# Moving the small steps of a softmax from ACT and GpSimd to VectorE, from the fourth block on

## The chip, the cores and the metric

The kernel runs on one core of a Trainium2 chip. The core has five engines, each with its own queue of instructions that it works off strictly in order: TensorE (PE in the profile; its weight loads are PEld) multiplies matrices and writes into PSUM, VectorE (DVE) and ScalarE (ACT) read and write SBUF and PSUM, GpSimd (POOL) works on SBUF, and SyncE (SP) issues the transfers (DMA). An instruction that needs another engine's result waits on a semaphore at the head of its queue, and everything behind it in that queue waits too. The metric is the time of one execution on the device in microseconds, lower is better.

## The reference, cut to what matters

```python
def sm(a, b):                                   # scale = 1/sqrt(128)
    s = scale * (a @ b.transpose(0, 2, 1))
    s = s - s.max(-1, keepdims=True)
    e = np.exp(s)
    return e / (e.sum(-1, keepdims=True) + 1e-09)
agent_v = sm(agents, k) @ v                     # 49 agents, 12480 tokens, width 128
x = sm(q, agents) @ agent_v                     # per token: a softmax over 49 scores
h = x @ w_in                                    # 128 -> 2048
g = np.where(h > 0.0, h, np.exp(np.minimum(h, 0.0)) - 1.0)
y = g @ w_out                                   # 2048 -> 128
h2 = y @ w_in2
out = (np.maximum(h2, 0.0) + alpha * np.minimum(h2, 0.0)) @ w_out2
```

All inputs and outputs are float32. The change concerns the softmax over the 49 scores of each token, `sm(q, agents)`.

## The kernel before

A prologue (about the first 70 us) computes `agent_v` and decodes the weights. It folds `agent_v` into the first weight matrix, so that the first layer takes the softmax's 49 weights directly. After that the tokens go through in 25 blocks (`BLOCKS`): block 0 of 384 tokens, six of 480 and eighteen of 512. The 2048 hidden features are 16 groups of 128, taken two at a time, so a block is 8 units. A loop `slot` takes two units per turn; a block is four turns.

For exactness each matmul operand is split into a high part in a shorter format and a low rest: `gh` and `gl`, `yh` and `yl`, `xh` and `xl`. Three matmuls (`mm3`, lines 436 to 438: high times high, high times low, low times high) make one product. For a unit pair `s`, `s+1` the stages are:

- `g1` (L602, L605): first layer, softmax weights `pst`, `psq` to `h`, in PSUM.
- `g1_act` (L612, L613) on ACT: `e`, in two passes. `g1_elu` (L620, and L622 for the first unit) on VectorE: `g`, and for the first unit also `gh`.
- `g1_split`: for the second unit the cast `gh` on ACT (L629); for both `gl = g - gh` on GpSimd (L631).
- `g2`: `y` from `gh` and `gl`, two units behind `g1`. At a block's end `yh` on ACT (L649), `yl` on VectorE (L650).
- `g3`: `h` of the second layer from `yh` and `yl`; `xh` on ACT (L661), `xl` on VectorE (L662). `g4`: the output `o`, ten units behind.

`h` of `g1`, `h` of `g3` and the scores take turns in three PSUM buffers (`hps`). A buffer is free again when VectorE has read it for `g` or `xl`; a matmul that is to write it waits for that.

The softmax of a coming block runs between these stages, in small steps, one to a quarter of a turn; the table `Q_STEPS` says at which quarter each is written. The scores stand as 64 rows (49 and padding) by tokens. `q_turn` transposes them in squares of 32, so that a token's scores lie along a row in two halves of 32 partitions each. `q_max` reduces each half (L185) and copies the second half's maxima beside the first (`m2`, L186, ACT). `q_less` takes the larger (`mx`, L194, VectorE), copies it to the second half (L195, ACT), and subtracts (`d`, L196, GpSimd). `q_exp` (L204, ACT) follows. `q_norm_1` and `q_norm_2` sum the halves (L211, L219, VectorE); `q_norm_3` adds the sums and 1e-9 (L225, L226, GpSimd); `q_norm_4` takes the reciprocal (L233, VectorE) and copies it to the second half (`r`, L234, ACT); `q_weigh` multiplies (L242, GpSimd). The small steps hold 32 partitions by 12 to 16 numbers.

Up to unit 12 (block 0 and half of block 1) a scheduler orders the instructions, and the steps for blocks 1 and 2 fall for the most part there. From unit 12 on, at about 150 us, the order on each engine is that in which the code is written (`tc.manual_schedule()`), one block like the next.

Of the kernel before, what the change touches and what calls it, by code (L numbers as in the profile page):

```python
# [12 lines left out]
ALU = mybir.AluOpType  # L13
# [12 lines left out]
L2 = 10  # L26
Q0 = 17
Q_AHEAD = 24
GBUFS = 4
XBUFS = 3  # L30
NY = 2
# [24 lines left out]
def agent_attention_moe_kernel(  # L56
# [26 lines left out]
    nc = tc.nc  # L83
# [51 lines left out]
    def qtile(tag, dtype=F32, part=AP):  # L135
        return sm.tile([P, BLK], dtype, tag=tag, name=tag)[:part]

    def qsmall(tag):
        return sm.tile([AP, BLK // 32], F32, tag=tag, name=tag)

    def by32(x, n):
        return x[:, :n].rearrange("p (j i) -> p j i", i=32)
# [37 lines left out]
    def q_max(b):  # L180
        n = blocks[b][1]
        st = q_st[b]
        j = n // 32
        m, m2 = qsmall("m"), qsmall("m2")
        nc.vector.tensor_reduce(out=m[:, :j], in_=by32(st, n), axis=AX.X, op=ALU.max)  # L185
        nc.scalar.copy(out=m2[:32, :j], in_=m[32:, :j])  # L186
        q_st[b] = st, m, m2

    def q_less(b):
        n = blocks[b][1]  # L190
        st, m, m2 = q_st[b]
        j = n // 32
        mx, d = qsmall("mx"), qtile("d")
        nc.vector.tensor_tensor(out=mx[:32, :j], in0=m[:32, :j], in1=m2[:32, :j], op=ALU.max)  # L194
        nc.scalar.copy(out=mx[32:, :j], in_=mx[:32, :j])  # L195
        nc.gpsimd.tensor_tensor(  # L196
            out=by32(d, n), in0=by32(st, n), in1=mx[:, :j].unsqueeze(2).to_broadcast([AP, j, 32]), op=ALU.subtract
        )
        q_st[b] = d
# [14 lines left out]
    def q_norm_2(b):  # L214
        n = blocks[b][1]
        e, s = q_st[b]
        j = n // 32
        s2 = qsmall("s2")
        nc.vector.tensor_reduce(out=s[32:, :j], in_=by32(e[32:], n)[:, :, :A - 32], axis=AX.X, op=ALU.add)  # L219
        q_st[b] = e, s, s2  # L220

    def q_norm_3(b):
        j = blocks[b][1] // 32
        e, s, s2 = q_st[b]
        nc.gpsimd.tensor_scalar(out=s2[:32, :j], in0=s[32:, :j], scalar1=1e-9, scalar2=None, op0=ALU.add)  # L225
        nc.gpsimd.tensor_tensor(out=s2[:32, :j], in0=s[:32, :j], in1=s2[:32, :j], op=ALU.add)  # L226
        q_st[b] = e, s2

    def q_norm_4(b):
        j = blocks[b][1] // 32  # L230
        e, s2 = q_st[b]
        r = qsmall("r")
        nc.vector.reciprocal(out=r[:32, :j], in_=s2[:32, :j])  # L233
        nc.scalar.copy(out=r[32:, :j], in_=r[:32, :j])  # L234
        q_st[b] = e, r

    def q_weigh(b):
# [21 lines left out]
    def q_place(b):  # L259
# [5 lines left out]


    Q_STEPS = {
        -3: [q_split], 3: [q_scores], 4: [q_sum, q_add], 6: [q_turn], 8: [q_max], 10: [q_less], 12: [q_exp],
        13: [q_norm_1], 14: [q_norm_2], 15: [q_norm_3], 16: [q_norm_4], 17: [q_weigh], 18: [q_turn], 19: [q_hi],
        21: [q_lo, q_place],  # L270
    }

# [320 lines left out]
    def wide(tag, dtype, n, bufs=WORK):  # L593
        return work.tile([P, 2, BLK], dtype, tag=tag, bufs=bufs, name=tag)[:, :, :n]
# [20 lines left out]
    def g1_elu(u):  # L615
        n = of(u)[2]
        g = wide("g", F32, n)
        gh = wide("gh", F32R, n, GBUFS)
        e, h = e_t.pop(u), h_t.pop(u)
# [5 lines left out]
    def g1_split(u):  # L625
        n = of(u)[2]
        g, gh = g_t[u]
        if u % 2 or u < AUTO:
            nc.scalar.copy(out=gh, in_=g)  # L629
        gl = wide("gl", F32R, n, GBUFS)  # L630
        nc.gpsimd.tensor_tensor(out=gl, in0=g, in1=gh.bitcast(F32), op=ALU.subtract)  # L631
# [65 lines left out]
    def queries(t):  # L697
# [3 lines left out]
        for c in range(max(1, b), min(b + 3, NB)):  # L701
            for k in range(-NF, Q_AHEAD - NF) if t == 0 and c == 1 else ():
                for f in Q_STEPS.get(k, ()):
                    f(c)
            for f in Q_STEPS.get(t - NF * c + Q_AHEAD, ()):
                f(c)
# [85 lines left out]
```

## Time and profile before

| what | value |
|---|---|
| median of 3 runs | 1144.31 us (1144.21 to 1144.8) |
| profiled execution | 1143.96 us |
| its span, first to last instruction | 1142.2 us |
| TensorE busy | 1080.3 us, 95% |
| ACT busy | 816.1 us, 71% |
| VectorE busy | 755.5 us, 66% |
| GpSimd busy | 623.1 us, 55% |
| mean granted TensorE clock | 0.987 of 2.4 GHz; 0.88 up to 133 us, 1.00 after it |
| one block of 512 tokens, from one L156 (802.46) to the next (844.80) | 42.34 us |

Busy times are shares of the span; the engines overlap. In a timeline a row gives the start, the duration, engine, line, operation and tiles; a bracket at its end gives how long the engine stood idle before it, and what it waited for. A matmul's duration includes its way through the array, and the next starts before it ends; what a matmul costs TensorE is the step from its start to the next one's.

### The profile page before, as it was taken

The numbers are of one execution on the slowest core, as the hardware profiler recorded it, in microseconds if no ns is written. First come the engines' busy times: TensorE is split into PE (matmuls) and PEld (weight loads), VectorE is DVE, ScalarE is ACT, GpSimd is POOL, SyncE is SP. The second block draws the span as 40 slices with busy tenths as digits, with TensorE's granted clock in tenths as the row PEclk, the third lists the DMA queues.
The fourth block names the chain that finished last, engine by engine and source line by source line (L and its number), as shares of the span: only waits on it lengthen the run. The fifth ranks groups of instructions, "written<-read, shape, count | busy, mean of one in ns | idle before, by whom it ended". The sixth has DMA issues, their size and how long they took to land.

```text
span 1142.2 us, 13519 instructions
## 1 busy us (share of the span) xinstructions
PE 1080.3 (95%) x5028; PEld 839.7 (74%) x5028; DVE 755.5 (66%) x861; ACT 816.1 (71%) x1014; POOL 623.1 (55%) x390
## 2 busy tenths in 40 slices
PE   7876999999999999999999999999999999999998
PEld 7835877778777777777777777777777777777776
DVE  7986656766666666766766665675675666667653
ACT  4469667777776776776777777777777777777763
POOL 3448555555565565655555565565555555555540
PEclk9977999999999999999999999999999999999999
DMA  9930000000000000000000010010000010000000
GB/s 361 302 114 18 18 8 18 27 9 19 27 18 19 19 18 20 19 21 18 19 28 10 19 29 10 19 29 10 19 28 10 19 29 10 19 19 10 19 1 19
DMA packets 28980, 41.35 MB, mean 36 GB/s; under 512 B 3329, under 2 KB 18511, under 8 KB 28915
## 3 DMA queue, kind: packets, MB, share of 16 engines
q1 hardware_dynamic: 28915, 40.49, 11.7%
q8 instruction: 40, 0.66, 0.2%
q14 instruction: 25, 0.20, 0.1%
HBM read 27.60 MB, written 6.39 MB: 30 GB/s over the span
## 4 chain that ended last, share of the span: by engine, by line
PE 43%; POOL 19%; ACT 16%; issue 10%; DVE 7%; DMA 1%; SPq 0%; POOLq 0%; DVEq 0%; ACTq 0%
POOL gl L631 16%; PE y L437 5%; PE h L436 5%; PE h L437 4%; PE h L438 4%; PE o L436 4%; PE y L438 4%; ACT gh L629 4%; ACT e L613 4%; PE y L436 4%; PE o L437 3%; PE o L438 3%; ACT xh L661 3%; ACT e L612 3%; PE h L602 3%
## 5 line engine op out<-in xcount | busy, mean ns | idle before, releaser
L631 POOL TENSOR_TENSOR gl<-g,gh 128x1024 fp32r<-128x1024 f32 (+2 forms) x200 | 468.8, 2344 | 354.5 <-ACT gh L629 168.8
L662 DVE SCALAR_TENSOR_TENSOR xl<-h,xh 128x1024 fp32r<-128x1024 f32 (+2 forms) x200 | 239.0, 1195 | 229.0 <-ACT xh L661 227.4
L620 DVE SCALAR_TENSOR_TENSOR g<-e,h 128x1024 f32<-128x1024 f32 (+2 forms) x200 | 236.1, 1181 | 82.8 <-ACT e L613 77.4
L661 ACT ACTIVATE xh<-h 128x1024 fp32r<-128x1024 f32 (+2 forms) x200 | 200.8, 1004 | 74.1 <-PE h L438 72.8
L613 ACT ACTIVATE e<-e 128x1024 f32<-128x1024 f32 (+2 forms) x200 | 207.8, 1039 | 6.0
L612 ACT ACTIVATE e<-h 128x1024 f32<-128x1024 f32 (+2 forms) x200 | 198.1, 991 | 10.3 <-PE h L605 10.2
L437 PE MATMUL y<-gl,wo1h 128*128 128x512 f32 (+2 forms) x400 | 158.2, 396 | 29.6 <-POOL gl L631 29.5
L436 PE MATMUL o<-xh,wo2h 128*128 128x512 f32 (+2 forms) x400 | 164.7, 412 | 0.0
L436 PE MATMUL h<-yh,wi2h 128*128 128x512 f32 (+2 forms) x400 | 156.7, 392 | 3.0 <-ACT yh L649 3.0
L437 PE MATMUL h<-yl,wi2h 128*128 128x512 f32 (+2 forms) x400 | 156.5, 391 | 2.9 <-DVE yl L650 1.3
L436 PE MATMUL y<-gh,wo1h 128*128 128x512 f32 (+2 forms) x400 | 156.2, 390 | 0.5 <-ACT gh L629 0.5
L438 PE MATMUL y<-gh,wo1l 128*128 128x512 f32 (+2 forms) x400 | 154.9, 387 | 0.0
L437 PE MATMUL o<-xl,wo2h 128*128 128x512 f32 (+2 forms) x400 | 154.1, 385 | 0.8 <-DVE xl L662 0.8
L438 PE MATMUL o<-xh,wo2l 128*128 128x512 f32 (+2 forms) x400 | 154.4, 386 | 0.0
L438 PE MATMUL h<-yh,wi2l 128*128 128x512 f32 (+2 forms) x400 | 154.4, 386 | 0.0
L437 PEld LDWEIGHTS y<-gl,wo1h 128*128 128x128 f32 x400 | 75.8, 190 | 54.1 <-POOL gl L631 39.8
L622 DVE SCALAR_TENSOR_TENSOR gh<-e,h 128x1024 fp32r<-128x1024 f32 (+1 forms) x94 | 112.7, 1199 | 0.0
L602 PE MATMUL h<-pst,s 128*128 128x512 f32 (+2 forms) x400 | 109.8, 395 | 2.9 <-POOL gl L631 2.0
L629 ACT CAST gh<-g 128x1024 fp32r<-128x1024 f32 (+2 forms) x106 | 107.6, 1015 | 2.0 <-DVE g L620 1.1
L436 PEld LDWEIGHTS o<-xh,wo2h 128*128 128x128 f32 x400 | 74.9, 187 | 34.4 <-issue 20.8
L436 PEld LDWEIGHTS h<-yh,wi2h 128*128 128x128 f32 x400 | 75.0, 188 | 25.6 <-DVE g L620 7.7
L437 PEld LDWEIGHTS h<-yl,wi2h 128*128 128x128 f32 x400 | 75.1, 188 | 25.0 <-DVE yl L650 11.8
(142 smaller groups left out, 1238.7 us busy)
## 6 DMA issues: line engine op xcount, KB each, us to landing
vt<-in_vm_dram SPq DMA_DIRECT2D x9, 640.0 KB
kt<-in_kT_dram SPq DMA_DIRECT2D x8, 640.0 KB
q<-in_qT_dram SPq DMA_DIRECT2D x18, 256.0 KB
psq<-pst SPq DMA_DIRECT2D x72, 64.0 KB
out_dram<-o SPq DMA_DIRECT2D x18, 256.0 KB
wi<-in_w_in_dram SPq DMA_DIRECT2D x8, 512.0 KB
wo<-in_w_out_dram SPq DMA_DIRECT2D x8, 512.0 KB
q<-in_qT_dram SPq DMA_DIRECT2D x6, 240.0 KB
```

The costliest lines, as they stand in the source:

```text
L436: nc.tensor.matmul(out, w_hi, x_hi, start=start, stop=False)
L437: nc.tensor.matmul(out, w_hi, x_lo, start=False, stop=False)
L438: nc.tensor.matmul(out, w_lo, x_hi, start=False, stop=stop)
L602: nc.tensor.matmul(h_t[u + v][:, c, :], s1[:, i + 2 * v + c, :], pst[b][:, :n], start=True, stop=False)
L612: nc.scalar.activation(out=e, in_=h_t[u], func=AF.Relu, scale=-1.0)
L613: nc.scalar.activation(out=e, in_=e, func=AF.Exp, scale=-1.0)
L620: nc.vector.scalar_tensor_tensor(out=g, in0=e, scalar=-1.0, in1=h, op0=ALU.add, op1=ALU.max)
L622: nc.vector.scalar_tensor_tensor(out=gh, in0=e, scalar=-1.0, in1=h, op0=ALU.add, op1=ALU.max)
L629: nc.scalar.copy(out=gh, in_=g)
L631: nc.gpsimd.tensor_tensor(out=gl, in0=g, in1=gh.bitcast(F32), op=ALU.subtract)
L661: nc.scalar.activation(out=xh, in_=h, func=AF.Relu)
L662: nc.vector.scalar_tensor_tensor(out=xl, in0=h, scalar=0.0, in1=xh.bitcast(F32), op0=ALU.max, op1=ALU.subtract)
```

## The change

For blocks below `Q_FIRST = 3` nothing is computed elsewhere. From block 3 on `m2`, the second half of `mx`, and the second half of `r` are made by VectorE instead of by a copy on ACT (the second half of `mx` by taking the maximum twice). The two additions of `q_norm_3` become a copy of `s2` and one fused operation on VectorE. In `Q_STEPS` the steps `q_less`, `q_exp` and `q_norm_1` move one quarter forward, for all blocks.

```diff
+Q_FIRST = 3
     def q_max(b):
-        nc.scalar.copy(out=m2[:32, :j], in_=m[32:, :j])
+        (nc.scalar.copy if b < Q_FIRST else nc.vector.tensor_copy)(out=m2[:32, :j], in_=m[32:, :j])
     def q_less(b):
-        nc.vector.tensor_tensor(out=mx[:32, :j], in0=m[:32, :j], in1=m2[:32, :j], op=ALU.max)
-        nc.scalar.copy(out=mx[32:, :j], in_=mx[:32, :j])
+        for h in range(2):
+            if h and b < Q_FIRST:
+                nc.scalar.copy(out=mx[32:, :j], in_=mx[:32, :j])
+                continue
+            nc.vector.tensor_tensor(out=mx[32 * h:32 * h + 32, :j], in0=m[:32, :j], in1=m2[:32, :j], op=ALU.max)
     def q_norm_2(b):
         nc.vector.tensor_reduce(out=s[32:, :j], in_=by32(e[32:], n)[:, :, :A - 32], axis=AX.X, op=ALU.add)
+        if b >= Q_FIRST:
+            nc.vector.tensor_copy(out=s2[:32, :j], in_=s[32:, :j])
     def q_norm_3(b):
-        nc.gpsimd.tensor_scalar(out=s2[:32, :j], in0=s[32:, :j], scalar1=1e-9, scalar2=None, op0=ALU.add)
-        nc.gpsimd.tensor_tensor(out=s2[:32, :j], in0=s[:32, :j], in1=s2[:32, :j], op=ALU.add)
+        if b < Q_FIRST:
...
+        else:
+            nc.vector.scalar_tensor_tensor(
+                out=s2[:32, :j], in0=s[:32, :j], scalar=1e-9, in1=s2[:32, :j], op0=ALU.add, op1=ALU.add
+            )
     def q_norm_4(b):
-        nc.scalar.copy(out=r[32:, :j], in_=r[:32, :j])
+        (nc.scalar.copy if b < Q_FIRST else nc.vector.tensor_copy)(out=r[32:, :j], in_=r[:32, :j])
     Q_STEPS = {
-        ... 8: [q_max], 10: [q_less], 12: [q_exp], 13: [q_norm_1], 14: [q_norm_2], ...
+        ... 8: [q_max], 9: [q_less], 11: [q_exp], 12: [q_norm_1], 14: [q_norm_2], ...
```

The diff adds lines, so in the order of the changed kernel lines 196 to 219 stand 4 further down, and those from 233 on 11 (L662 is L673, L629 is L640, L661 is L672).

The order of ACT in a block of 512 tokens, around the copy `r` (L234). Before:

```order
L682 COPY o<-o 128x512
L148 CAST qh<-q 128x512
L661 ACTIVATE xh<-h 128x1024
L234 COPY r<-r 32x16
L629 CAST gh<-g 128x1024
```

Now:

```order
L693 COPY o<-o 128x512
L149 CAST qh<-q 128x512
L672 ACTIVATE xh<-h 128x1024
L640 CAST gh<-g 128x1024
L672 ACTIVATE xh<-h 128x1024
```

The copy `r` is gone from ACT, and the cast `gh` follows `xh`. The copies `m2` (L186) and `mx` (L195) are gone in the same way from two other places of the block.

VectorE around the reciprocal, before:

```order
L622 SCALAR_TENSOR_TENSOR gh<-e,h 128x1024
L219 TENSOR_REDUCE s<-d 32x16
L620 SCALAR_TENSOR_TENSOR g<-e,h 128x1024
L662 SCALAR_TENSOR_TENSOR xl<-h,xh 128x1024
L233 RECIPROCAL r<-s_6145 32x16
L662 SCALAR_TENSOR_TENSOR xl<-h,xh 128x1024
```

Now:

```order
L633 SCALAR_TENSOR_TENSOR gh<-e,h 128x1024
L223 TENSOR_REDUCE s<-d 32x16
L225 COPY s_6145<-s 32x16
L631 SCALAR_TENSOR_TENSOR g<-e,h 128x1024
L673 SCALAR_TENSOR_TENSOR xl<-h,xh 128x1024
L235 SCALAR_TENSOR_TENSOR s_6145<-s,s_6145 32x16
L244 RECIPROCAL r<-s_6145 32x16
L245 COPY r<-r 32x16
L673 SCALAR_TENSOR_TENSOR xl<-h,xh 128x1024
```

`s_6145` is the program's `s2`. Its copy stands in front of a `g`, and the fused addition and the copy `r` stand around the reciprocal, in front of an `xl`.

VectorE around the maxima, before:

```order
L662 SCALAR_TENSOR_TENSOR xl<-h,xh 128x1024
L185 TENSOR_REDUCE m<-st 64x16
L662 SCALAR_TENSOR_TENSOR xl<-h,xh 128x1024
L620 SCALAR_TENSOR_TENSOR g<-e,h 128x1024
L622 SCALAR_TENSOR_TENSOR gh<-e,h 128x1024
L194 TENSOR_TENSOR mx<-m,m_5997 32x16
L620 SCALAR_TENSOR_TENSOR g<-e,h 128x1024
L650 TENSOR_TENSOR yl<-y,yh 128x512
```

Now:

```order
L673 SCALAR_TENSOR_TENSOR xl<-h,xh 128x1024
L186 TENSOR_REDUCE m<-st 64x16
L187 COPY m_5997<-m 32x16
L673 SCALAR_TENSOR_TENSOR xl<-h,xh 128x1024
L199 TENSOR_TENSOR mx<-m,m_5997 32x16 x2
L631 SCALAR_TENSOR_TENSOR g<-e,h 128x1024
L633 SCALAR_TENSOR_TENSOR gh<-e,h 128x1024
L631 SCALAR_TENSOR_TENSOR g<-e,h 128x1024
L661 TENSOR_TENSOR yl<-y,yh 128x512
```

The copy `m2` (`m_5997`) stands behind the reduction, and the two maxima stand in front of `g` and `gh` instead of between `gh` and the next `g`. On GpSimd, L225 and L226 are gone and the subtraction `d` (L196) moves ahead of one `gl`; on TensorE and SP the order is the same as before, and so is that of the scheduled part.

## Rows read from the trace of the kernel before

**Rows 1.** The page's first part: each engine's busy time, share of the span, instructions.

```profile
PE 1080.3 (95%) x5028; PEld 839.7 (74%) x5028; DVE 755.5 (66%) x861; ACT 816.1 (71%) x1014; POOL 623.1 (55%) x390
```

**Rows 2.** Waits, 150 to 1050 us: who waited, total us, times, longest us.

```profile
PE y L437 <- POOL gl L631: 25.9, 21, 1.6
...
PEld h L437 <- DVE yl L650: 11.8, 22, 0.7
PEld h L436 <- DVE g L620: 7.7, 21, 0.5
```

**Rows 3.** Timeline of TensorE: start us, us, engine, line, operation, idle before.

```profile
838.95 0.39 PE L438 MATMUL y<-gh,wo1l 128*128 128x512 f32 x1
839.18 0.39 PE L436 MATMUL y<-gh,wo1h 128*128 128x512 f32 x1
840.82 0.50 PE L437 MATMUL y<-gl,wo1h 128*128 128x512 f32 x1 [1.25 <-POOL gl L631]
841.16 0.40 PE L438 MATMUL y<-gh,wo1l 128*128 128x512 f32 x1
```

**Rows 4.** Timeline of TensorE, two other places of the same block.

```profile
822.68 0.39 PE L436 MATMUL h<-yh,wi2h 128*128 128x512 f32 x1
823.18 0.50 PE L437 MATMUL h<-yl,wi2h 128*128 128x512 f32 x1
...
845.03 0.40 PE L157 MATMUL h<-ql,ag 128*128 128x512 f32 x1
845.39 0.50 PE L436 MATMUL h<-yh,wi2h 128*128 128x512 f32 x1
```

**Rows 5.** Timeline of ACT in the same block.

```profile
837.04 0.20 ACT L234 COPY r<-r 32x16 f32<-32x16 f32 x1 [3.68 <-DVE r L233]
837.26 1.05 ACT L629 CAST gh<-g 128x1024 fp32r<-128x1024 f32 x1
```

**Rows 6.** Timeline of GpSimd in the same block.

```profile
832.46 1.30 POOL L149 TENSOR_TENSOR ql<-q,qh 128x512 fp32r<-128x512 f32 x1 [3.51 <-ACT qh L148]
833.72 2.39 POOL L631 TENSOR_TENSOR gl<-g,gh 128x1024 fp32r<-128x1024 f32 x1
...
838.38 2.38 POOL L631 TENSOR_TENSOR gl<-g,gh 128x1024 fp32r<-128x1024 f32 x1 [1.65 <-ACT gh L629]
```

**Rows 7.** Timeline of VectorE in the same block.

```profile
831.81 0.43 DVE L219 TENSOR_REDUCE s<-d 32x16 f32<-32x272 f32 x1
832.26 1.22 DVE L620 SCALAR_TENSOR_TENSOR g<-e,h 128x1024 f32<-128x1024 f32 x1
...
836.77 0.24 DVE L233 RECIPROCAL r<-s 32x16 f32<-32x16 f32 x1 [2.15 <-POOL s L226]
```

**Rows 8.** The groups of the whole run, line 194: total us, mean ns.

```profile
L194 DVE TENSOR_TENSOR mx<-m,m 32x16 f32<-32x16 f32 (+2 forms) x25 | 4.5, 179 | 0.6 <-ACT m L186 0.6
```

**Rows 9.** Timeline of ACT, later in the block.

```profile
839.12 1.01 ACT L612 ACTIVATE e<-h 128x1024 f32<-128x1024 f32 x1
...
856.97 0.20 ACT L186 COPY m<-m 32x16 f32<-32x16 f32 x1 [1.87 <-DVE m L185]
...
859.07 1.01 ACT L612 ACTIVATE e<-h 128x1024 f32<-128x1024 f32 x1
```

**Rows 10.** Timeline of TensorE, two groups of L605.

```profile
835.88 0.51 PE L605 MATMUL h<-psq,s1q 32*128 32x512 f32 x4
...
857.62 0.51 PE L605 MATMUL h<-psq,s1q 32*128 32x512 f32 x4
```

**Rows 11.** Timeline of VectorE, yl and a g.

```profile
822.45 0.67 DVE L650 TENSOR_TENSOR yl<-y,yh 128x512 fp32r<-128x512 f32 x1
...
844.16 1.17 DVE L620 SCALAR_TENSOR_TENSOR g<-e,h 128x1024 f32<-128x1024 f32 x1
```

**Rows 12.** Timeline of VectorE, early in the run.

```profile
81.61 0.43 DVE L194 TENSOR_TENSOR mx<-m,m 32x15 f32<-32x15 f32 x1
```

**Rows 13.** Timeline of GpSimd, early in the run.

```profile
80.74 1.27 POOL L385 TENSOR_TENSOR wi2l<-dg,wi2h 128x512 fp32r<-128x512 f32 x1
```

More of the change, by code (lines that the diff above doesn't have):

```diff
@@ L224, in q_norm_3 @@
         e, s, s2 = q_st[b]
-        nc.gpsimd.tensor_scalar(out=s2[:32, :j], in0=s[32:, :j], scalar1=1e-9, scalar2=None, op0=ALU.add)
-        nc.gpsimd.tensor_tensor(out=s2[:32, :j], in0=s[:32, :j], in1=s2[:32, :j], op=ALU.add)
+        if b < Q_FIRST:
+            nc.gpsimd.tensor_scalar(out=s2[:32, :j], in0=s[32:, :j], scalar1=1e-9, scalar2=None, op0=ALU.add)
+            nc.gpsimd.tensor_tensor(out=s2[:32, :j], in0=s[:32, :j], in1=s2[:32, :j], op=ALU.add)
+        else:
+            nc.vector.scalar_tensor_tensor(
+                out=s2[:32, :j], in0=s[:32, :j], scalar=1e-9, in1=s2[:32, :j], op0=ALU.add, op1=ALU.add
+            )
         q_st[b] = e, s2
@@ L267, in agent_attention_moe_kernel @@
     Q_STEPS = {
-        -3: [q_split], 3: [q_scores], 4: [q_sum, q_add], 6: [q_turn], 8: [q_max], 10: [q_less], 12: [q_exp],
-        13: [q_norm_1], 14: [q_norm_2], 15: [q_norm_3], 16: [q_norm_4], 17: [q_weigh], 18: [q_turn], 19: [q_hi],
+        -3: [q_split], 3: [q_scores], 4: [q_sum, q_add], 6: [q_turn], 8: [q_max], 9: [q_less], 11: [q_exp],
+        12: [q_norm_1], 14: [q_norm_2], 15: [q_norm_3], 16: [q_norm_4], 17: [q_weigh], 18: [q_turn], 19: [q_hi],
         21: [q_lo, q_place],
```

## The prediction

> **What bounds the kernel now.** I read the page's engine line first, then the table of waits for TensorE, then the timelines of one block, engine by engine. TensorE is busy for 95% of the span, GpSimd for 55%, VectorE for 66% and ACT for 71% [rows 1]; so the order of the matmuls sets the time, and only what holds TensorE up can be won. From 150 to 1050 us three waits come back about once in each block [rows 2]: y L437 for gl from GpSimd (21 times), h L437 for yl (22 times), h L436 for the buffer that g on VectorE gives back (21 times). What each costs I take from the block at 820 to 862 us, from one start to the next. The matmuls start every 0.23 us there (838.95 to 839.18), but the one after 839.18 starts at 840.82: 1.64 in place of 0.23, so 1.41 is lost, and 0.11 more in the step after it (0.34) [rows 3]. The yl wait: 822.68 to 823.18 is 0.50, so 0.27 is lost. The wait for g: 845.03 to 845.39 is 0.36, so 0.13 is lost [rows 4]. After both I count the same 0.11. The sum is 1.52 + 0.38 + 0.24 = 2.14 us in a block of 512 tokens.
>
> **Why TensorE waits for gl.** gl is computed on GpSimd at 838.38, 2.38 long, after the cast gh on ACT at 837.26 [rows 5, 6]. That cast's input g was there at 833.48 (832.26 + 1.22, [rows 7]). ACT stood idle for 3.68 us before 837.04, since the 0.20 us copy r L234 is queued in front of the cast and waits for the reciprocal L233 [rows 5]. The reciprocal waited 2.15 for L226 on GpSimd [rows 7], and L225 and L226 are queued behind the gl that started at 833.72 and ended at 836.11 [rows 6]. So a chain DVE, GpSimd, DVE, ACT over 32x16 numbers delays a cast that TensorE needs.
>
> **The change part by part.** In 22 blocks (3 to 24) ACT loses three copies (m2, mx, r; about 0.2 each) and GpSimd two small operations. VectorE loses nothing and gains five: the m2 copy, the second max, the s2 copy, one fused add, the r copy. The nearest row is the max L194 at 179 ns on average [rows 8], so I charge 0.15 to 0.25 each, some 1 us of VectorE per block, 22 us on 755.5 busy: it stays far from the bound. TensorE's and SP's orders do not change, nor do the DMAs.
>
> *The r chain.* In the new order ACT's cast follows xh directly, so it can start about when g is ready, 833.5. It ends near 834.6. GpSimd is then still in the gl of 833.72, so the second gl starts at 836.1 and ends at 838.5; TensorE wants it at 839.41 (839.18 + 0.23). The 1.52 goes with 0.9 to spare, 0.5 if the yl wait has gone too and TensorE is 0.38 earlier. What is late next would be this same gl, by GpSimd's own two gl in a row.
>
> *The m2 and mx copies.* At 856.97 ACT stood idle for 1.87 before the copy m2 L186, with a cast, xh and L612 behind it. L612 starts at 859.07 although its h was ready at 858.13 (857.62 + 0.51) [rows 9, 10]: 0.94 late. L613, g, gh, g and yl follow one after another, so yl, which starts at 822.45 in the block shown [rows 11] and holds TensorE up for 0.38, comes some 0.9 earlier: the 0.38 goes, with 0.5 to spare. The subtraction d and the exp now stand a quarter slot earlier, before a gl in GpSimd's queue; the maxima stand before a g that waits for L613 anyway (L612, which L613 follows, starts at 859.07 [rows 9]), so I cost that step at nothing. If that cover failed, g would be later by the length of what blocks the maxima.
>
> *The wait for g.* L612 starts at 839.12 with its h ready at 836.39 (835.88 + 0.51), 2.73 late, because of the same r copy [rows 9, 10]; it feeds g at 844.16 [rows 11]. TensorE will come there 1.52 earlier against that h, and needs another 0.24: 1.76 of the 2.73. So this wait goes as well, with about 1 us of room, less what VectorE itself is held up.
>
> **What can hold VectorE up.** At 81.61 the max L194, which reads two tiles in SBUF, took 0.43 us in place of 0.18, and ended at 82.04; GpSimd's operation of 80.74 ended at 82.01 [rows 8, 12, 13]. VectorE waited for it, and the next operation of GpSimd did not get in first. So a small step that meets a gl can cost up to the rest of that gl, 2.4 us at most; at least it costs its own 0.15. I walk the five through the block on that footing. The m2 copy meets a gl and delays the xl behind it by about 0.8; that xl is not wanted for some microseconds. The maxima follow that gl, with GpSimd idle until d. The s2 copy comes at 832.24 (831.81 + 0.43, [rows 7]), before ql starts at 832.46 [rows 6]: free by 0.2 us only. The fused add, the reciprocal and the r copy meet the two gl in a row, so r is ready about when the second ends, and the xl behind them is 1.5 to 2 us late; of this the g of the next pair feels about 0.5, which leaves 0.5 of the room named above. None reaches TensorE in the likeliest case.
>
> The Trainium skill (SBUF — State Buffer, Who interferes with whom) states this as an exclusive lock: a VectorE copy in a two-port mode, or an operation with two SBUF inputs, and a GpSimd operation that reads SBUF exclude each other for a whole instruction. By that rule all five added steps are exposed; the row at 81.61 agrees, and it speaks against this change.
>
> **The sum.** 21 blocks with all three waits give 21 x 2.14 = 44.9 us; block 24 has no gl wait (21 of them), but its yl wait gives at least 0.38. The blocks of 480 tokens are among the 21 and I take them alike. The profiled execution took 1143.96 us (span 1142.2 and 1.8 around it): 1143.96 - 45.3 = 1098.7. The median of the runs is 0.35 higher, so 1099.0. I keep back 1 us for small steps that are late by less than they were: **1100**.
>
> **The rivals.**
> 1. *Only the gl wait goes.* VectorE, held by GpSimd, hands yl and the h buffer over as late as before. Against it: the room of 0.5 each; for it: that room is thin. 21 x 1.52 = 31.9 us: 1112.
> 2. *The s2 copy meets ql.* It lies 0.2 us before ql in the rows, and ACT's copy qh, which releases ql, will come earlier too. It then waits until 833.76 (832.46 + 1.30), 1.52 later. The g and xl behind it are 1.5 later; the third of the four matmuls L602 in front of 835.88 (two steps of 0.23 earlier, 835.4) needs the buffer that this xl frees, near 836.2 (832.26 + 1.52 and 1.22 each for g and xl). It costs 0.8 a block: 21 x (2.14 - 0.8) = 28: 1116.
> 3. *Slower.* The same copy loses against ql and then against the gl behind it: until 836.11 (833.72 + 2.39), 3.87 late. xl ends near 838.6 by the same working, and TensorE loses 3.2 in a block where it gains 2.14: 21 x 1.06 = 22 us: 1166. The change becomes a loss as soon as TensorE stands more than 2.14 there. Against it: at 82.0 the waiting VectorE came before the next GpSimd operation.
> 4. *No change.* The gl is late by GpSimd's own queue, so that the order of the casts decides nothing: 1144. Against it: GpSimd was idle before 838.38, and the row names ACT's gh as what released it.
>
> **How the numbers follow.** Forecast 0.72 (its own range 1097 to 1106), rival 1 0.13, rival 2 0.07, rival 3 0.04, rival 4 0.04. The range of 8 in 10 runs from 1097, all stalls gone and nothing kept back, with some for the fills I did not count, to 1113, which takes in rival 1. A change under 0.2%, 2.3 us, can't be told from none. Faster: 0.72 + 0.13 + 0.07 = 0.92; the same 0.04; slower 0.04.
>
> **What would show it.** The block's period falls from 42.34 us (from one L156 to the next) to near 40.2. The row y L437 <- gl nearly vanishes after 170 us. ACT shows no 3.7 us gap before the cast and no 1.9 us gap. VectorE's small steps read 0.15 to 0.25 where GpSimd is idle and up to 2.4 where it is not. I am wrong if TensorE waits for g or xl in each block by more than a few tenths, or if the period stays above 41.

## The result, and the profile after

The changed kernel takes 1097.67 us (median of 4 runs, 1097.47 to 1099.03) against 1144.31 before: a ratio of 0.9594 with a 95% interval of 0.9578 to 0.9611. The forecast was 1100, its range 1097 to 1113; the sum before the 1 us that was kept back was 1099.0.

The profiled execution was the slowest of the four, 1099.03 us with a span of 1097.2. The mean granted TensorE clock is 0.86 of 2.4 GHz up to 136 us and 1.00 after it, where it had been 0.88 up to 133 us and 1.00 after it; so in the blocks from 3 on the clock is the same. Its engine line, beside [rows 1]:

```profile
PE 1066.0 (97%) x5028; PEld 849.2 (77%) x5028; DVE 852.6 (78%) x971; ACT 812.3 (74%) x948; POOL 614.2 (56%) x346
```

TensorE is busy for 97% instead of 95%. ACT and GpSimd lose 4 and 9 us of work. VectorE gains 97 us where 22 had been charged; that is the number of the forecast that is furthest off, and most of it is waiting (below).

Of the three waits of [rows 2] one entry of 0.3 us is left, and one for an xl (0.5) is new; it comes up again with the rivals. This is TensorE's whole table of waits from 150 to 1050 us (the matmuls themselves have none, these are weight loads); the columns are as in [rows 2]. The first three entries, at L616 and at the first o, stood at the same loads before, with 30.5 and 20.3 us:

```profile
PEld h L616 <- issue: 32.1, 91, 0.4
PEld o L447 <- ACT xh L672: 16.9, 70, 0.2
PEld o L447 <- issue: 5.1, 21, 0.2
PEld h L613 <- DVE xl L673: 0.5, 1, 0.5
PEld h L448 <- DVE yl L661: 0.3, 1, 0.3
```

The place of [rows 3] in the block at 809 to 849 us. The matmul with gl (L448) follows 0.23 us after the one before it, where it had been 1.64:

```profile
844.70 0.39 PE L449 MATMUL y<-gh,wo1l 128*128 128x512 f32 x1
844.92 0.39 PE L447 MATMUL y<-gh,wo1h 128*128 128x512 f32 x1
845.15 0.39 PE L448 MATMUL y<-gl,wo1h 128*128 128x512 f32 x1
845.38 0.39 PE L449 MATMUL y<-gh,wo1l 128*128 128x512 f32 x1
```

Two score matmuls, one block apart: the period is 40.15 us, where it had been 42.34 (L157 is the old L156).

```profile
808.86 0.39 PE L157 MATMUL h<-qh,ag 128*128 128x512 f32 x1
...
849.01 0.39 PE L157 MATMUL h<-qh,ag 128*128 128x512 f32 x1
```

ACT, which answers to [rows 5]: the copy r is gone and the cast gh follows xh without a gap. L672 is xh, L640 the cast, L623 the first pass for e. Between the last two rows ACT now waits for TensorE (0.33), not for VectorE:

```profile
838.12 1.03 ACT L672 ACTIVATE xh<-h 128x1024 fp32r<-128x1024 f32 x1 [1.24 <-PE h L449]
839.04 1.04 ACT L640 CAST gh<-g 128x1024 fp32r<-128x1024 f32 x1
840.84 1.03 ACT L672 ACTIVATE xh<-h 128x1024 fp32r<-128x1024 f32 x1 [0.76 <-PE h L449]
842.21 1.03 ACT L623 ACTIVATE e<-h 128x1024 f32<-128x1024 f32 x1 [0.33 <-PE h L616]
```

VectorE, which answers to [rows 7]. The s2 copy is free (0.16), the fused addition L235 takes 0.33, and the copy r takes 2.04:

```profile
836.82 0.16 DVE L225 COPY s<-s 32x16 f32<-32x16 f32 x1
...
840.32 0.33 DVE L235 SCALAR_TENSOR_TENSOR s<-s,s 32x16 f32<-32x16 f32 x1
840.68 0.24 DVE L244 RECIPROCAL r<-s 32x16 f32<-32x16 f32 x1
840.96 2.04 DVE L245 COPY r<-r 32x16 f32<-32x16 f32 x1
843.03 1.23 DVE L673 SCALAR_TENSOR_TENSOR xl<-h,xh 128x1024 fp32r<-128x1024 f32 x1
```

GpSimd beside it: two gl, 4.76 us together, end at 842.97. The copy r ends at 843.00 and sa, which needs r, starts at 843.14:

```profile
838.21 4.76 POOL L642 TENSOR_TENSOR gl<-g,gh 128x1024 fp32r<-128x1024 f32 x2
843.14 1.05 POOL L253 TENSOR_TENSOR sa<-d,r 64x512 f32<-64x512 f32 x1 [0.17 <-DVE r L245]
```

So VectorE stands for two microseconds in a copy of 16 numbers per partition, behind GpSimd, as the row at 81.61 [rows 12] had shown on a smaller scale; the xl behind it starts at 843.03 instead of about 841.9, when xh was there (840.84 + 1.03). TensorE does not wait for it. The five steps as groups of the whole run (the old L194 stands in [rows 8]), with count, total us and mean ns:

```profile
L245 DVE COPY r<-r 32x16 f32<-32x16 f32 (+1 forms) x22 | 44.3, 2015 | 0.8
...
L187 DVE COPY m<-m 32x16 f32<-32x16 f32 (+1 forms) x22 | 32.3, 1469 | 0.8
...
L199 DVE TENSOR_TENSOR mx<-m,m 32x16 f32<-32x16 f32 (+2 forms) x47 | 8.6, 184 | 0.9 <-ACT m L187 0.6
...
L235 DVE SCALAR_TENSOR_TENSOR s<-s,s 32x16 f32<-32x16 f32 (+1 forms) x22 | 7.3, 333 | 0.0
...
L225 DVE COPY s<-s 32x16 f32<-32x16 f32 (+1 forms) x22 | 6.4, 293 | 0.8
```

They sum to 98.9 us, where the old max alone had 4.5: 94 of the 97 us. (L199 counts the 25 old maxima too.)

### The profile page after: what moved, and what is told of

Read it like the earlier page. It is cut to its first block, busy times and chain, and to the rows that moved or that the text cites. A ratio compares the mean times of both kernels' runs of the same rounds, so it can differ in the third digit from the quotient of the medians.

```text
span 1097.2 us, 13474 instructions
## 1 busy us (share of the span) xinstructions
PE 1066.0 (97%) x5028; PEld 849.2 (77%) x5028; DVE 852.6 (78%) x971; ACT 812.3 (74%) x948; POOL 614.2 (56%) x346
## 4 chain that ended last, share of the span: by engine, by line
PE 88%; ACT 2%; DVE 2%; POOL 1%; DMA 1%; issue 0%; SPq 0%; POOLq 0%; ACTq 0%; DVEq 0%
PE o L447 10%; PE o L449 8%; PE o L448 8%; PE h L613 8%; PE h L447 8%; PE h L448 8%; PE h L449 8%; PE y L447 8%; PE y L448 8%; PE y L449 8%; PE h L616 4%; DMA al<-in_alpha_dram 1%; POOL gl L642 1%; ACT e L624 1%; ACT e L623 1%; PE h L157 1%
## 5 line engine op out<-in xcount | busy, mean ns | idle before, releaser
L673 DVE SCALAR_TENSOR_TENSOR xl<-h,xh 128x1024 fp32r<-128x1024 f32 (+2 forms) x200 | 239.6, 1198 | 125.8 <-ACT xh L672 124.3
L672 ACT ACTIVATE xh<-h 128x1024 fp32r<-128x1024 f32 (+2 forms) x200 | 201.2, 1006 | 176.8 <-PE h L449 176.3
L623 ACT ACTIVATE e<-h 128x1024 f32<-128x1024 f32 (+2 forms) x200 | 199.1, 996 | 30.4 <-PE h L616 29.4
L448 PE MATMUL y<-gl,wo1h 128*128 128x512 f32 (+2 forms) x400 | 156.5, 391 | 2.2 <-POOL gl L642 2.2
L447 PE MATMUL h<-yh,wi2h 128*128 128x512 f32 (+2 forms) x400 | 154.4, 386 | 2.3 <-ACT yh L660 2.3
L448 PE MATMUL o<-xl,wo2h 128*128 128x512 f32 (+2 forms) x400 | 153.8, 384 | 0.8 <-DVE xl L673 0.8
L448 PE MATMUL h<-yl,wi2h 128*128 128x512 f32 (+2 forms) x400 | 154.4, 386 | 0.0
L613 PE MATMUL h<-pst,s 128*128 128x512 f32 (+2 forms) x400 | 111.1, 398 | 2.4 <-POOL gl L642 1.9
L640 ACT CAST gh<-g 128x1024 fp32r<-128x1024 f32 (+2 forms) x106 | 107.4, 1013 | 2.6 <-DVE g L631 2.6
L613 PEld LDWEIGHTS h<-pst,s 128*128 128x128 f32 x400 | 76.7, 194 | 19.9 <-issue 3.0
L448 PEld LDWEIGHTS y<-gl,wo1h 128*128 128x128 f32 x400 | 76.5, 191 | 17.7 <-POOL gl L642 3.2
L150 POOL TENSOR_TENSOR ql<-q,qh 128x512 fp32r<-128x512 f32 (+2 forms) x25 | 31.6, 1264 | 102.0 <-ACT qh L149 97.9
```

What stands on the lines that cost most here:

```text
L447: nc.tensor.matmul(out, w_hi, x_hi, start=start, stop=False)
L448: nc.tensor.matmul(out, w_hi, x_lo, start=False, stop=False)
L613: nc.tensor.matmul(h_t[u + v][:, c, :], s1[:, i + 2 * v + c, :], pst[b][:, :n], start=True, stop=False)
L623: nc.scalar.activation(out=e, in_=h_t[u], func=AF.Relu, scale=-1.0)
L672: nc.scalar.activation(out=xh, in_=h, func=AF.Relu)
L673: nc.vector.scalar_tensor_tensor(out=xl, in0=h, scalar=0.0, in1=xh.bitcast(F32), op0=ALU.max, op1=ALU.subtract)
```

## The experiments

All were compared with the kernel before, on the same chip. There its median was 1145.3 to 1146.1, some 0.1% above the first measurement, so gains are told as ratios. Three theories stood against each other. *Queue*: TensorE's waits come from small copies that stand at the head of ACT's and GpSimd's queues and wait for VectorE. *Exclusion*: as the queue theory, but VectorE's small steps wait for GpSimd's running operation, and this decides where they pay. *Places*: the gain is from the table, in which d and exp stand one quarter earlier.

### 1. The sums' part alone

m2 and mx on ACT, old table; the rest as in the changed kernel.

```diff
-        (nc.scalar.copy if b < Q_FIRST else nc.vector.tensor_copy)(out=m2[:32, :j], in_=m[32:, :j])
+        nc.scalar.copy(out=m2[:32, :j], in_=m[32:, :j])
-            if h and b < Q_FIRST:
+            if h:
-    ... 9: [q_less], 11: [q_exp], 12: [q_norm_1], ...
+    ... 10: [q_less], 12: [q_exp], 13: [q_norm_1], ...
```

> The sums' part alone from block 3 on (s2 copy, fused addition and copy r on VectorE); m2 and mx stay on ACT and the steps keep their old places. Queue theory: the gl wait (1.52 us a block) and the wait for g (0.24) go, the yl wait (0.38) stays, because L186 and L195 still hold ACT up: 1144 - 21 x 1.76 = 1107. Rival (places theory: what wins is that d and exp stand one quarter earlier): next to nothing, 1140 to 1144.

Measured: 1112.42 us, ratio 0.9714 (0.9700 to 0.9729). The gl wait is gone from TensorE's table but for 0.5 us in one block; the yl wait stays as it was (11.8 us, 22 times, as in [rows 2]), as expected. The places theory (1140 or more) cannot be the whole cause, for here the table is the old one. It misses 1107 because the wait for g stays too:

```profile
PEld h L448 <- DVE yl L661: 11.8, 22, 0.7
PEld h L447 <- DVE g L631: 6.4, 19, 0.7
```

The queue theory has no reason for that, the exclusion has one. The fused addition meets the first gl and the copy r the second, 1.43 and 2.06 us. From there VectorE has no idle time up to the g of 654.41, which ends at 655.58, and TensorE, which could have gone on at 655.27, waits 0.36 us for it:

```profile
646.55 1.43 DVE L235 SCALAR_TENSOR_TENSOR s<-s,s 32x16 f32<-32x16 f32 x1
...
648.28 2.06 DVE L245 COPY r<-r 32x16 f32<-32x16 f32 x1
...
655.63 0.19 PEld L447 LDWEIGHTS h<-yh,wi2h 128*128 128x128 f32 x1 [0.36 <-DVE g L631]
```

### 2. The maxima's part with the new table

```diff
-            nc.vector.tensor_copy(out=s2[:32, :j], in_=s[32:, :j])
...
-        (nc.scalar.copy if b < Q_FIRST else nc.vector.tensor_copy)(out=r[32:, :j], in_=r[:32, :j])
+        nc.scalar.copy(out=r[32:, :j], in_=r[:32, :j])
```

The additions of q_norm_3 stay on GpSimd for all blocks.

> The maxima's part (m2 and mx on VectorE from block 3 on) with the steps moved a quarter forward; the sums' steps and r stay on GpSimd and ACT. Queue theory in its simple form: only the yl wait goes, 1144 - 22 x 0.38 = 1136. By a walk through the block, ACT's earlier exp also brings qh, ql, the gl of the pair's first unit and so L225, L226 and r forward by some 1.6 us, so that the gl wait nearly vanishes though r stays on ACT, and the wait for g grows to about 0.6: 1144 - 21 x 1.5 = 1113. Places theory: near 1100.

Measured: 1110.00 us, 0.9691 (0.9676 to 0.9705). The simple queue theory (1136) falls: r is still on ACT, yet TensorE's weight loads wait for gl 9.8 us instead of 35.2. First the row of the kernel before, which [rows 2] leaves out, then the two of this run:

```profile
PEld y L437 <- POOL gl L631: 35.2, 22, 2.0
...
PEld y L446 <- POOL gl L640: 9.8, 21, 0.7
PEld h L445 <- DVE g L629: 7.5, 21, 0.4
```

The walk through the block comes near (1113) and is right on gl, but not on g: that wait did not grow (7.5 us here, 7.7 in [rows 2]). The places theory (near 1100) falls as well.

### 3. The table alone

```diff
-    ... 8: [q_max], 10: [q_less], 12: [q_exp],
-    13: [q_norm_1], ...
+    ... 8: [q_max], 9: [q_less], 11: [q_exp],
+    12: [q_norm_1], ...
```

> Only the table of steps (q_less, q_exp, q_norm_1 a quarter earlier, all blocks); every operation stays on its old engine. Simple queue theory: all three small copies still stand in ACT's queue, 1136 to 1144. Places theory: d stands ahead of a gl, the exp is 2 us earlier, what follows on ACT is earlier by about 1.4 us, and the gl wait loses most of its 1.52: about 1115 to 1120.

Measured: 1116.52 us, 0.9751 (0.9736 to 0.9766): 28.8 us less with no operation on another engine, as the places theory said. TensorE's weight loads:

```profile
PEld y L437 <- POOL gl L631: 10.5, 22, 0.8
PEld h L437 <- DVE yl L650: 10.4, 22, 0.9
```

The yl wait stays, the gl wait is less than a third of its 35.2. ACT shows how: the copy r still waits, 2.43 us instead of 3.68, but it comes earlier against TensorE: the exp L204, for which ACT had waited 1.7 us a block for d (the first row, of the kernel before), now starts without a wait in all 22 blocks (the rows behind it), and all that follows on ACT moves forward:

```profile
824.90 0.63 ACT L204 ACTIVATE d<-d 64x512 f32<-64x512 f32 x1 [1.74 <-POOL d L196]
...
638.04 0.62 ACT L204 ACTIVATE d<-d 64x512 f32<-64x512 f32 x1
...
651.21 0.20 ACT L234 COPY r<-r 32x16 f32<-32x16 f32 x1 [2.43 <-DVE r L233]
```

### 4. The engines alone

The changed kernel with the old table.

> All small steps on VectorE from block 3 on, but at their old places in the table. Queue theory without the exclusion between VectorE and GpSimd: 1098 to 1101, as with the moved steps. With it: the two maxima stand between gh and the next g, where gl starts 0.15 us after gh ends; if the second maximum starts after that gl, it waits 2.3 us for it, g and yl come that much later, TensorE loses some 1.8 us a block there in place of 0.38, and the time is about 1098 + 21 x 1.8 = 1135. If both maxima win the race, 1100. Places theory: 1110 or above.

Measured: 1099.54 us, 0.9598 (0.9582 to 0.9614), the changed kernel's ratio. The places theory falls as the cause of this result: with the small steps on VectorE the table is worth nothing that the measured times can tell. The traces show 1.6 us for it (from the score matmul of block 3 to the end 962.8 here and 961.2 in the changed kernel). The two maxima won their race against the gl, 0.34 us for both, so the 1135 did not come:

```profile
626.22 0.34 DVE L199 TENSOR_TENSOR mx<-m,m 32x16 f32<-32x16 f32 x2
```

What the table does give is room. Here the g that experiment 1 had late ends at 648.73, 0.18 us before TensorE's load at 648.91; in the changed kernel it ends at 848.49, 0.75 before the load at 849.24.

### 5. The copy r alone on VectorE

```diff
-        nc.scalar.copy(out=r[32:, :j], in_=r[:32, :j])
+        (nc.scalar.copy if b < 3 else nc.vector.tensor_copy)(out=r[32:, :j], in_=r[:32, :j])
```

> Only the copy r goes from ACT to VectorE from block 3 on; the additions stay on GpSimd, the table of steps is the old one. ACT's cast gh is then free of the chain. Without exclusion between VectorE and GpSimd: gl wait and wait for g go, 1144 - 21 x 1.76 = 1107. With it: the copy r follows the reciprocal at 837.0, when GpSimd has begun the next gl (about 836.8 to 839.15); VectorE waits some 2.1 us in the copy, the xl and both g behind it are late, and the wait for g grows from 0.24 to some 0.9: 1144 - 21 x 0.86 = 1126.

Measured: 1125.06 us, 0.9823 (0.9808 to 0.9837): the exclusion's 1126, not the queue theory's 1107. The gl wait has gone from TensorE's table but for 0.8 us of weight loads in two blocks, and in its place TensorE waits for g:

```profile
PE h L436 <- DVE g L620: 10.0, 21, 0.7
```

VectorE stands in the copy (L234) for 2.09 us:

```profile
615.73 0.24 DVE L233 RECIPROCAL r<-s 32x16 f32<-32x16 f32 x1 [2.11 <-POOL s L226]
616.00 2.09 DVE L234 COPY r<-r 32x16 f32<-32x16 f32 x1
```

GpSimd had taken the next gl at 615.66, before the reciprocal began, and held it to 618.06; the copy ended at 618.09:

```profile
615.66 2.40 POOL L631 TENSOR_TENSOR gl<-g,gh 128x1024 fp32r<-128x1024 f32 x1
```

### 6. The additions alone on VectorE

s2 copy and fused addition on VectorE, r on ACT, m2 and mx on ACT, old table. What is added to the kernel before (the additions on GpSimd stay for blocks below 3):

```diff
+        if b >= Q_FIRST:
+            nc.vector.tensor_copy(out=s2[:32, :j], in_=s[32:, :j])
...
+            nc.vector.scalar_tensor_tensor(
+                out=s2[:32, :j], in0=s[:32, :j], scalar=1e-9, in1=s2[:32, :j], op0=ALU.add, op1=ALU.add
+            )
```

> Only the additions of q_norm_3 go from GpSimd to VectorE (s2 copy and fused addition) from block 3 on; r stays a copy on ACT, the table of steps is the old one. Without exclusion: the reciprocal ends near 835.2, the cast is ready at 836.6, the gl wait goes: about 1112. With it: the fused addition meets the gl of 833.72 and ends after 836.1, the copy r at 836.8, the cast at 837.9, and the gl wait only shrinks from 1.5 to about 1.1 us: 1144 - 21 x 0.4 = 1136.

Measured: 1134.96 us, 0.9908 (0.9892 to 0.9925): again the exclusion's number (1136, not 1112). The fused addition (L235) takes 1.42 us, ending with the gl of 619.58 to 621.98:

```profile
620.58 1.42 DVE L235 SCALAR_TENSOR_TENSOR s<-s,s 32x16 f32<-32x16 f32 x1
622.03 0.24 DVE L244 RECIPROCAL r<-s 32x16 f32<-32x16 f32 x1
```

ACT's copy r still waits 3.10 us, and TensorE for gl 14.0 us in 21 times (25.9 in [rows 2]):

```profile
622.31 0.20 ACT L245 COPY r<-r 32x16 f32<-32x16 f32 x1 [3.10 <-DVE r L244]
```

### 7. The three copies without the exclusion

The copies of the changed kernel as reductions over a length of one (s2 shown, m2 and r alike).

```diff
-            nc.vector.tensor_copy(out=s2[:32, :j], in_=s[32:, :j])
+            nc.vector.tensor_reduce(out=s2[:32, :j], in_=s[32:, :j].unsqueeze(2), axis=AX.X, op=ALU.max)
```

> The changed kernel with its three copies on VectorE (m2, s2, r) written as a reduction over a length of one, which reads one tile and is no copy. If the 1.55 us of the m2 copy and the 2.05 of the copy r are waits for GpSimd, they fall to 0.15 to 0.25, and VectorE's busy time falls from 853 by 22 x (1.4 + 1.85) = 71 to about 780 us; TensorE, which waits for none of it, keeps its 40.15 us a block: 1096 to 1099. If these durations belong to the operation itself (32 partitions, shifted), they stay, and so does 853.

Measured: 1097.18 us, 0.9582 (0.9567 to 0.9596). The same numbers are moved beside the same gl in 0.16 us; m2 is L190, r L251:

```profile
618.48 0.16 DVE L190 TENSOR_REDUCE m<-m 32x16 f32<-32x16 f32 x1
...
638.59 0.16 DVE L251 TENSOR_REDUCE r<-r 32x16 f32<-32x16 f32 x1
```

GpSimd was in a gl each time (617.62 to 620.01, and two from 635.84 to 640.62). VectorE is busy for 70 us less than in the changed kernel:

```profile
PE 1062.5 (97%) x5028; PEld 847.9 (77%) x5028; DVE 782.6 (71%) x971; ACT 812.2 (74%) x948; POOL 613.4 (56%) x346
```

So the 1.55 and 2.05 us were waits for GpSimd, and TensorE did not need the time that they cost: the 21 intervals between the score matmuls of blocks 3 to 24 sum to 833.3 us here and to 833.5 in the changed kernel.

### 8. VectorE held up on purpose

```diff
+            pad = qsmall("r")
+            for _ in range(12):
+                nc.vector.reciprocal(out=pad[:32, :j], in_=s[:32, :j])
```

> The changed kernel with twelve more reciprocals of 32x16 (0.24 each, about 3.1 us with the steps between) on VectorE behind the s2 copy in blocks 3 to 24; their results are not used. The g and xl behind them have 0.95 us of their own before xh is there and some 0.7 us before the third matmul of the next g1 needs the buffer: 3.1 of delay makes xl end near 842.5 in place of 840.4 in the block of the changed kernel at 830 to 844, with TensorE wanting it at 841.1. 1.4 x 22 = 31: about 1128. If VectorE's lateness does not reach TensorE through these buffers: 1098. If it reaches TensorE in full (no room at all): 1098 + 68 = 1166.

Measured: 1138.02 us, 0.9940 (0.9925 to 0.9954), 10 more than expected. The twelve take 3.27 us. TensorE stands in front of the group of matmuls that was named, but at two of its four: first for the buffer that g frees, which had not been expected, then for the one that xl frees (idle before, in brackets):

```profile
700.83 0.39 PE L452 MATMUL h<-yh,wi2l 128*128 128x512 f32 x1
701.83 0.74 PE L616 MATMUL h<-pst,s 128*128 128x512 f32 x2 [0.61 <-DVE g L634]
702.96 0.73 PE L616 MATMUL h<-pst,s 128*128 128x512 f32 x2 [0.40 <-DVE xl L676]
```

The period is 41.70 us, 1.55 above the changed kernel's 40.15 (1.4 expected). Beside experiment 7, which ran on the same chip, the 21 intervals between the score matmuls of blocks 3 to 24 cost 35.1 us more (868.4 against 833.3), 3.5 of them in the first (43.27 us against 39.81), and what comes behind the last of them 5.1 more (132.5 against 127.4). In that last stretch TensorE stands 2.55 us for g in place of 0.61: there the s2 copy in front of the twelve takes 2.10 us instead of 0.16, and the 1.94 come through in full. So once the room is used up, VectorE's lateness reaches TensorE one for one, and the room in this place is 3.27 - 1.55 = 1.7 us, the 0.95 for xh and the 0.7 together.

### 9. The candidates

The changed kernel again, the version of experiment 7 again, and that version with `Q_FIRST = 2` and `Q_FIRST = 1`, side by side.

```diff
-Q_FIRST = 3
+Q_FIRST = 2
```

> The changed kernel itself, beside the three below on the same chip: 1097 to 1099.

> The version whose three copies are reductions over a length of one, again: TensorE has no wait left that VectorE could shorten, so the time is that of the changed kernel within 1 us. If the waits of VectorE for GpSimd cost something in blocks in which the s2 copy meets ql (two of 22 in the changed kernel's trace), 0.5 to 2 us less.

> The same with Q_FIRST = 2, so block 2 too has its small steps on VectorE. Its gl and yl waits fall in the scheduled part or just behind it (150 us): at best one block's 2.1 us less, 1095; as the scheduler there orders the matmuls anew, it can as well lose 2 to 5 us: 1100.

> The same with Q_FIRST = 1, blocks 1 and 2 too. At best two blocks' 2.1 us less, 1093; the scheduled part gets another order of matmuls, in which block 1's first units come earlier between those of block 0: 1093 to 1105.

Measured: 1097.91 (0.9580, 0.9566 to 0.9593), 1097.25 (0.9573, 0.9560 to 0.9586), 1098.10 (0.9579, 0.9566 to 0.9592) and 1098.07 us (0.9582, 0.9569 to 0.9595). None can be told from the changed kernel. The version without the copies had the lower median both times, by 0.5 us (experiment 7, measured apart from the changed kernel) and 0.7 us (here, side by side), which is within the intervals. The traces show 0.4 of it: behind the last score matmul the changed kernel takes 127.8 and 127.7 us in its two traces, this version 127.4 in both. The reason is in block 24 (below, with the rivals). In the measured times no version is shown to be better.

## Why the prediction was right

**The bound and the three waits.** Right: the waits of [rows 2] are gone, and the order of the matmuls sets the period. Per block of 512 tokens the gain is 42.34 - 40.15 = 2.19 us, for 2.14 in the sum. Over the 21 intervals between score matmuls from the first that the change can reach to the last, TensorE needs 833.5 us (135.99 to 969.45) instead of 880.4 (133.75 to 1014.11): 46.9 for 44.9. The 0.05 a block makes about 1 us in the blocks of 512 tokens. Three intervals near the start and where the block size changes gained 2.4 to 3.0 us, and four of 480 tokens only 1.9 to 2.1; all had been taken like the others. Behind the last score matmul 0.3 us came (128.1 to 127.8) where 0.38 had been charged. The 1 us kept back was not lost. The profiled run was 2.2 us later than the one before at the score matmul of block 3 (135.99 against 133.75), with the same order of instructions up to there, so this is not the change. That the profiled spans differ by 45.0 us, so near the 45.3 of the sum, is therefore partly luck: 46.9 + 0.3 - 2.2. It probably is also why the profiled run took 1099.03 and the median is 1097.67; the other runs have no trace that would show it.

**The r chain.** Right in its end, too simple in its cause. Experiment 6 shows that freeing GpSimd alone leaves most of the gl wait, and experiment 5 that freeing ACT alone removes it, as predicted. But experiment 3 removes most of it with r left on ACT. The wait is the end of a longer chain (d, exp, L612, qh, ql, the pair's first gl, L225, r, the cast); it can be cut at more than one place, and the cuts do not add: 28.8 us for the table, 45.8 for the engines, and 46.6 and 48.2 for both, in the two measurements.

**The table at nothing.** The sum costed it so, and experiment 4 agrees: beside the moved engines it is worth 1.6 us in the traces, less than the measured times can tell. That it would be worth 28.8 us by itself the prediction did not see: it walked only the order in which both parts change together.

**The m2 copy and yl.** Right: the yl wait stays in 1, 3, 5 and 6, where m2 is on ACT (10.4 to 11.9 us of weight loads), and goes in 2, 4 and 7 (0.3 to 0.9).

**VectorE's price.** The term that was mis-sized. It charged 0.15 to 0.25 us for each step, 22 us in all; 97 came. The walk behind it had the waits nearly right: 0.8 us for the xl behind m2, where 0.7 came (822.44 instead of 821.71, when its xh was there), and 1.5 to 2 behind r, where 1.2 came. But the sum of busy time left them out. The copy m2 takes 1.55 and r 2.04, and these two cost TensorE nothing, which experiment 7 shows directly.

**The rivals.** That only the gl wait goes did not come about, and neither did no change: the gl was late by the casts' order, as experiment 5 shows. The race of the s2 copy against ql was as close as the prediction feared: in 20 of the 22 blocks the copy starts 0.05 to 0.16 us before ql. Twice it met GpSimd. In the block at 676 it took 1.10 us, until ql ended at 677.66:

```profile
676.59 1.10 DVE L225 COPY s<-s 32x16 f32<-32x16 f32 x1
```

```profile
676.37 1.29 POOL L150 TENSOR_TENSOR ql<-q,qh 128x512 fp32r<-128x512 f32 x1 [4.33 <-ACT qh L149]
```

The gl behind ql, which starts at 677.62, did not hold it. The delay is 0.94 us, and TensorE's period in that block is 40.15 like the others. In block 24, the last, no ql comes, and the copy meets the gl itself:

```profile
997.41 2.10 DVE L225 COPY s<-s 32x16 f32<-32x16 f32 x1
```

```profile
1001.95 0.30 PEld L613 LDWEIGHTS h<-pst,s 128*128 128x128 f32 x2 [0.52 <-DVE xl L673]
```

There the delay is 1.94 us, more than the room of 1.7 that experiment 8 found, and TensorE does stand, at the matmul and for the xl that rival 2 named; that is the one new entry in its table. From the first L613 to L616 it needs 1.38 us instead of 1.01, so it loses 0.4. In experiment 7 this is absent, and the stretch behind the last score matmul is 0.4 us shorter. So the way in which rivals 2 and 3 would lose time exists, but it opens only beyond some 1.6 us (1.94 less what TensorE lost) and was met once (the expectation in experiment 9 took both meetings for ql); rival 2's price (0.8 for 1.5 us of delay) was too high.

**VectorE beside GpSimd.** In the changed kernel the long copies, and the fused additions that take more than 0.25 us, end 0.02 to 0.04 us after an instruction of GpSimd, and in experiment 7 a tensor_reduce runs beside one in 0.16 us. The Trainium skill's rule (SBUF — State Buffer, Who interferes with whom) agrees with both: a copy in a two-port mode and an operation with two inputs in SBUF are blocked to the end of a GpSimd instruction that reads SBUF and began first, and a tensor_reduce never contends with it on this chip.

## What to carry to other kernels

A tiny copy on an engine that waits for another engine costs what stands behind it in the queue; look for gaps before instructions of 0.2 us, and ask which engine already holds the data. When a wait ends a long chain, test each cut by itself: two that gained 29 and 46 us apart gained about 47 together. Before moving small steps to VectorE, look whether GpSimd is running there; if it is, a reduction over a length of one moves the same numbers without waiting. Whether that is worth anything depends on whether the engine that sets the time waits for what stands behind the step; here the traces show 0.4 us of 1097 for it.

## What the runs showed of the hardware

A VectorE copy of 32x16 numbers took 0.16 us when it began with GpSimd idle and 1.1 to 2.1 us when an operation of GpSimd had begun before it; in the changed kernel all 45 copies that took longer than 0.5 us ended 0.02 to 0.04 us after that operation. The profile counts this wait as busy time and names no releaser for it. Written as a reduction over a length of one, it took 0.16 us beside a running gl. A reciprocal of the same size took 0.24 us beside a running gl.
